# Reordering the head of a fused S5 scan and gated-MLP kernel: load order, held-back weights, tile-wise gate steps

## Chip, cores, metric

The kernel runs on one core of one Trainium2 chip. The metric is device time in microseconds for one execution. TensorE is called PE, VectorE DVE, ScalarE ACT, GpSimd POOL and SyncE SP; SP, ACT and POOL each have a queue on which they issue DMA transfers.

## What is computed

One input `x` of 2048 tokens by 448 channels is normalised; a diagonal complex state-space recurrence (S5) with 448 states runs over the tokens, and a gated MLP with 1792 hidden channels runs beside it. All arrays are bf16.

```python
xn = layernorm(x)                       # over the 448 channels, no scale or shift
# A: S5
dt = exp(log_dt); Lam_bar = exp(dt * Lam)
Bu = xn @ (((Lam_bar - 1) / Lam)[:, None] * B).T
h[t] = Lam_bar * h[t-1] + Bu[t]         # t = 0 .. 2047, complex
s = 2 * real(h @ C.T) + xn * Dskip
# B: gated MLP
g = silu((sigmoid(xn @ w_gate) * (xn @ w_up)) @ w_down)
out = x + s * g
```

## The kernel before

The 2048 tokens are 16 tiles of 128 tokens, in four chunks of 512. For each chunk the kernel does this:

- **Normalise** (`stats`, `chain`, `norm`): batch-norm statistics on DVE (L347, L348), then the reciprocal deviation. For chunk 0 that is a short chain over DVE and ACT (L356 to L359) and a DVE normalisation (L371) with a copy of the first 64 columns behind the last (the seam, L375). For later chunks the deviation is computed on POOL (L362 to L366), the normalisation is on ACT (L378) and the seam copy on POOL (L381).
- **Transpose**: for chunk 0 on PE, seven 128x128 transposes per tile (`pe_transpose`, L400), evacuated by ACT (L402) and DVE (L404) into `xnT`; for later chunks by two DMA transposes per tile on SP's queue (L307).
- **Gate and up steps** (`gu_step`): for each of seven blocks m, 14 matmuls of 64 rows by 512 tokens (L603, L604: both 64-row halves of the array). In chunk 0 all seven gate blocks come first, then the up blocks; a gate block is evacuated by ACT as a tanh (L619) and an up block by DVE (L628), into `hF`. In later chunks gate and up alternate (L622, L632 on ACT, L633 on DVE). Three PSUM slots `gu` go round.
- **Scan** (`b_units`, `ssm_pair`, `ssm_stack`): the input projections (L667) are copied out by ACT (L678), rotated by cosine and sine tables, scanned on DVE (L721, L753) and rotated back. The tables come from `tables`: phases on DVE (L472, L475, L477, L480), sines and cosines on ACT (L484, L486). The phases need `turn`, which `columns` computes from the four parameter vectors: loaded as rows, turned into columns by 16 one-column matmuls (L438), then ACT's exponential (L443) and small POOL steps (L449, L452).
- **Down and output** (`down`, `yout`): the down projection (L782), the output projection (L810), and the store of each tile.

The order of the work is made by a planner (`Plan`). Every piece of work is entered with its engine, a cost, the tiles it reads and those it writes. `solve` works out due times backwards from PE's order and then picks, for each engine, the available piece that is due first; `emit` issues the instructions in the order of planned start. PE's pieces, and the pieces marked `chain` (the loads of each queue), keep the order in which they were entered. So each engine's order is fixed when the kernel is built, and on the chip an engine waits at its next instruction even if a later one could run.

At the start (entered around L322), the loads are: on SP's queue x tiles 0, 1, then 2 and 3 together, two gate-weight blocks, three up-weight blocks, then x tiles 4 to 7 (`load_x(4, 4)`) and the transposed load of B; on ACT's queue two gate blocks and one up block, after a table load; on POOL's queue four vectors, the down weights `wd` and x tiles 8 to 15, each without a condition. The weights of a kind come as four loads: two halves of 64 partitions, each in a block of the first three m (336 KB) and one of the last four (448 KB). PE starts with 12 matmuls on a zero tile (`warm_mm`). Then tile 0 and tile 1 get gate steps of their own for the first three blocks (`g_head`), and tiles 2 and 3 a common one.

Of the kernel before, what the change touches and what calls it, by code (L numbers as in the profile page):

```python
# [18 lines left out]
D = 448  # L19
F = 1792  # L20
# [52 lines left out]
class Plan:  # L73
# [53 lines left out]
    def solve(self, pe_from):  # L127
# [11 lines left out]
        for o in reversed(self.ops):  # L139
            for b, kind in o.suc:  # L140
                x = b.late - self._gap(o, b, kind) - o.cost
                if kind is not None and o.eng != b.eng:
                    x -= 1.5 if o.dma else 0.2
                o.late = min(o.late, x)
# [38 lines left out]
def kernel(  # L183
# [73 lines left out]
    one = sb.tile([1, 1], BF16, name="one")  # L257
    pio2 = sbt("pio2", [1], FP32)
    vrow = hF_raw[0][0:1, 0:2048].rearrange("p (a b) -> p a b", a=4)
# [27 lines left out]
    def load(eng, key, nbytes, o, i, cost=0.45):  # L287
        e = {"SP": Q, "ACT": A, "POOL": G}[eng]
        add(eng, cost, lambda: e.dma_start(out=o, in_=i), w=[key] if not isinstance(key, list) else key,
            dma=nbytes, chain=True)  # L290

    def load_x(t0, n, q="SP"):
        load(q, [("x", t) for t in range(t0, t0 + n)], n * P * D * 2,
             x_all[:, t0:t0 + n, :], x_src[:, t0:t0 + n, :])
# [3 lines left out]
    def load_w(eng, k, half, b):  # L298
# [5 lines left out]
             wsrc[k][:, c0 + m0 * P:c0 + m1 * P].rearrange("(s p) f -> p s f", p=H))  # L304
# [5 lines left out]
    add("POOL", 0.3, lambda: G.memset(warm[:], 0.0), w=["warm"])  # L310
# [3 lines left out]
    add("POOL", 0.1, lambda: G.memset(one[:], 1.0), w=["one"])  # L314
# [6 lines left out]

    add("ACT", 1.3, lambda: A.preload_act_table_set("sqrt_and_others"), w=["sqrttab"], chain=True)  # L322
    load_x(0, 1)
    load_x(1, 1)
    load_x(2, 2)
    load_w("ACT", "g", 1, 0)
    load_w("SP", "g", 0, 0)
    load_w("ACT", "g", 1, 1)
    load_w("SP", "g", 0, 1)
    load_w("ACT", "u", 1, 0)  # L330
    load_w("SP", "u", 0, 0)
    load_w("SP", "u", 1, 1)
    load_w("SP", "u", 0, 1)
    for k, vec in enumerate((A_log_dt, A_Lambda_im, A_Lambda_re, A_Dskip)):
        load("POOL", ("vrow", k), D * 2, vrow[:, k, 0:448], vec.unsqueeze(0), cost=1.0)


    def warm_mm(n):
# [3 lines left out]
        add("PE", 0.35 * n, f, r=["warm"], w=[("gu", 2)])  # L342
# [7 lines left out]
    def chain(t0, n):  # L350
# [4 lines left out]
        if t0 < TPC:  # L355
            add("DVE", 0.09, lambda: V.tensor_single_scalar(out=ve, in_=var, scalar=EPS, op=ALU.add), r=ks("mv"), w=ks("ve"))  # L356
            add("ACT", 0.2, lambda: A.activation(sd, ve, ACT.Sqrt), r=ks("ve") + ["sqrttab"], w=ks("sd"))
            add("DVE", 0.09, lambda: V.tensor_copy(out=meanf[:, t0:t0 + n, :], in_=mean), r=ks("mv"), w=ks("mf"))
# [9 lines left out]
    def norm(t):  # L368
        b = t % NXN
        if t < TPC:  # L370
# [4 lines left out]
            add("DVE", 0.085, lambda: V.tensor_copy(out=xn[b][:, 448:512], in_=xn[b][:, 0:64]),  # L375
# [18 lines left out]
    def pe_transpose(t):  # L394
# [3 lines left out]
        def f():  # L398
            for s in range(7):
                T.transpose(tp[:, s, :], xn[b][:, s * H:s * H + P], ident[:, :])  # L400
        add("PE", 0.43, f, r=[("xn", b), ("xnw", b), "ident"], w=[("acc", a)])
        add("ACT", 0.476, lambda: A.copy(out=xnT[0][:, 0:4, js], in_=tp[:, 0:4, :]),  # L402
            r=[("acc", a)], w=[("xnT", 0, t, "a")])
        add("DVE", 0.27, lambda: V.tensor_copy(out=xnT[0][:, 4:7, js], in_=tp[:, 4:7, :]),  # L404
            r=[("acc", a)], w=[("xnT", 0, t, "b")])
# [23 lines left out]
    def columns():  # L429
        a = next_acc()  # L430
        vps = flat(acc[a][:, 0:16], 4, 4)
        add("POOL", 0.3, lambda: G.tensor_copy(out=vrow[:, :, 448:512], in_=vrow[:, :, 384:448]),
            r=[("vrow", k) for k in range(4)], w=["vroww"])

        def f():
            for k in range(4):
                for i in range(4):
                    T.matmul(vps[:, k, i:i + 1], lhsT=vrow[:, k, i * P:(i + 1) * P], rhs=one[:], start=True, stop=True)  # L438
        add("PE", 1.0, f, r=["vroww", "one"] + [("vrow", k) for k in range(4)], w=[("acc", a)])
        pv = sbt("pv", [4, 4], FP32)  # L440
        add("DVE", 0.1, lambda: V.tensor_copy(out=pv[:], in_=vps[:]), r=[("acc", a)], w=["pv"])
# [7 lines left out]
        tt = lambda o, x, y, op: (lambda: G.tensor_tensor(out=o, in0=x, in1=y, op=op))  # L449
        theta, arg, turn, r_col = C("theta"), C("arg"), C("turn"), C("r")  # L450
        pool(tt(theta[:], dt_b[:], lim, ALU.mult), ["dt", "pv"], ["theta"])
        pool(lambda: G.tensor_single_scalar(out=turn[:], in_=theta[:], scalar=1.0 / TWO_PI, op=ALU.mult),  # L452
# [538 lines left out]
```

## Time and profile before

| | |
|---|---|
| median of 2 runs | 207.5 us (206.95 to 208.05) |
| profiled execution | 206.59 us, its span 204.8 us |
| PE busy | 186.2 us, 91% of the span |
| DVE busy | 160.0 us, 78% |
| ACT busy | 114.6 us, 56% |
| POOL busy | 43.4 us, 21% |
| chain that ended last, by engine | PE 50%, DVE 23%, DMA 13%, ACT 5%, POOL 4% |
| read from HBM, written | 6.66 MB, 1.84 MB |

The profiled execution's time is its span and 1.8 us around it. Busy shares are means over the whole span. Times in views are counted from the start of the span. In the view by stretches a row gives, after the length, the busy time of PE, PE's weight load, DVE, ACT and POOL with instruction counts, then the granted PE clock as a share of full speed, the DMA share and GB/s. In the view by engine a row gives start, duration, engine, line, operation, the tile written and those read, and in brackets the idle time before it with what ended it.

### The profile page before, as it was taken

Reading aid. Unit: us, or ns where it says so; the run is one execution under the profiler, and the core shown is the slowest. Engines: PE = TensorE matmul, PEld = TensorE weight load, DVE = VectorE, ACT = ScalarE, POOL = GpSimd, SP = SyncE. Lnnn points to the kernel's source line nnn. Section 1 sums busy time; section 2 is a strip of 40 time slices with the busy share of each in tenths; the row PEclk is TensorE's granted clock in tenths of the full one; section 3 lists DMA queues with packets and bytes.
Section 4 is the critical chain, followed back from the end, with each engine's and each line's share of the span. In section 5 each row is a group of like instructions: output and inputs, shape, how many; then the busy total and the mean of one; then the engine's idle time right before and its main releaser. Section 6 shows DMA issues by size and latency. Waiting matters only on the chain.

```text
span 204.8 us, 3700 instructions
## 1 busy us (share of the span) xinstructions
PE 186.2 (91%) x1459; PEld 92.5 (45%) x1459; DVE 160.0 (78%) x304; ACT 114.6 (56%) x160; POOL 43.4 (21%) x94
## 2 busy tenths in 40 slices
PE   7267995899799999999699999999999999999992
PEld 2156652434344544444244544444445444455561
DVE  1552539999999999999999999995599799531153
ACT  2114947948999956734935943836537582510330
POOL 8130749677100017007106100000000000000000
PEclk9859999999999999999999999999999999999998
DMA  5999994345400013300311220000000000001002
GB/s 143 235 295 338 223 165 88 74 91 109 89 2 3 0 22 71 78 12 3 73 40 45 48 67 0 3 22 22 0 16 10 0 3 22 22 27 48 0 22 67
DMA packets 26946, 13.32 MB, mean 65 GB/s; under 512 B 19696, under 2 KB 26368, under 8 KB 26928
## 3 DMA queue, kind: packets, MB, share of 16 engines
q1 hardware_dynamic: 24800, 9.41, 21.6%
q0 software_dynamic: 736, 2.53, 3.9%
q10 hardware_dynamic: 1392, 1.15, 2.6%
q8 instruction: 11, 0.18, 0.4%
q14 instruction: 7, 0.06, 0.1%
HBM read 6.66 MB, written 1.84 MB: 41 GB/s over the span
## 4 chain that ended last, share of the span: by engine, by line
PE 50%; DVE 23%; DMA 13%; ACT 5%; POOL 4%; issue 2%; SPq 1%; DVEq 0%; POOLq 0%; ACTq 0%
PE gu L603 18%; DMA x_all<-in_A_x_dram 13%; PE acc L782 10%; PE acc L810 8%; PE gu L782 5%; PE gu L667 4%; DVE wv L721 4%; DVE hF L628 3%; DVE bst L347 2%; ACT sig L622 2%; DVE hF L633 2%; DVE cT L572 2%; POOL rsd L364 1%; PE acc L816 1%; POOL sdb L363 1%
## 5 line engine op out<-in xcount | busy, mean ns | idle before, releaser
L603 PE MATMUL gu<-xnT,wG 64*128 64x512 bf16 (+2 forms) x238 | 47.7, 347 | 5.0 <-DMA wG<-in_B_w_gate_dram 4.1
L603 PE MATMUL gu<-xnT,wU 64*128 64x512 bf16 x196 | 46.5, 376 | 2.4 <-ACT hF L619 2.4
L604 PE MATMUL gu<-xnT,wG 64*128 64x512 bf16 (+2 forms) x238 | 47.7, 347 | 0.0
L604 PE MATMUL gu<-xnT,wU 64*128 64x512 bf16 x196 | 46.5, 376 | 0.0
L782 PE MATMUL acc<-wd,hF 128*128 128x448 bf16 x168 | 33.8, 353 | 0.0
L603 PEld LDWEIGHTS <-wG 64*128 64x128 bf16 x238 | 21.4, 98 | 25.4 <-DMA wG<-in_B_w_gate_dram 4.2
L782 PEld LDWEIGHTS <-hF 128*128 128x128 bf16 x224 | 21.5, 98 | 21.3 <-issue 2.1
L622 ACT ACTIVATE sig<-gu 128x1024 bf16<-128x1024 f32 x21 | 21.5, 1022 | 14.5 <-PE gu L604 12.1
L603 PEld LDWEIGHTS <-wU 64*128 64x128 bf16 x196 | 17.9, 94 | 22.8 <-issue 2.1
L632 ACT CAST ub<-gu 128x1024 bf16<-128x1024 f32 x21 | 21.2, 1009 | 9.2 <-PE gu L604 9.1
L810 PE MATMUL acc<-cT,hT 128*128 128x448 bf16 x105 | 24.3, 353 | 0.0
L721 DVE TENSOR_TENSOR_SCAN wv<-c_r,st,z 128x512 bf16<-128x512 f32 x18 | 23.0, 1280 | 0.2
L604 PEld LDWEIGHTS <-wG 64*128 64x128 bf16 x238 | 21.1, 98 | 1.2 <-issue 1.0
L604 PEld LDWEIGHTS <-wU 64*128 64x128 bf16 x196 | 17.7, 94 | 3.3 <-issue 3.2
L633 DVE TENSOR_TENSOR hF<-sig,ub 128x1024 bf16<-128x1024 bf16 x21 | 14.2, 681 | 5.8 <-ACT ub L632 5.8
L347 DVE BATCH_NORM_STATS2 bst<-x_all 128x6 f32<-128x448 bf16 x16 | 9.4, 616 | 10.0 <-DMA x_all<-in_A_x_dram 10.0
L667 PE MATMUL gu<-xnT,bT 128*128 128x512 bf16 x72 | 16.9, 380 | 0.0
L792 DVE TENSOR_TENSOR g_t<-zb,sigd 128x448 bf16<-128x448 bf16 x16 | 6.1, 386 | 12.8 <-ACT zb L791 12.8
L678 ACT CAST bus<-gu 128x1024 bf16<-128x1024 f32 x12 | 12.1, 1010 | 4.8 <-PE gu L667 4.8
L810 PEld LDWEIGHTS <-hT 128*128 128x128 bf16 x119 | 10.4, 98 | 7.3 <-issue 0.4
L790 ACT ACTIVATE sigd<-acc 128x448 bf16<-128x448 f32 x12 | 6.5, 540 | 12.2 <-PE acc L782 12.2
L378 ACT ACTIVATE xn<-x_all,nmr,rsd 128x448 bf16<-128x448 bf16 x12 | 8.8, 754 | 5.6 <-POOL nmr L366 5.6
(140 smaller groups left out, 278.9 us busy)
## 6 DMA issues: line engine op xcount, KB each, us to landing
out_dram<-o_t SPq DMA_DIRECT2D x15, 112.0 KB, 1.7
wd<-in_B_w_down_dram POOLq DMA_DIRECT2D x1, 1568.0 KB, 13.6
wU<-in_B_w_up_dram SPq DMA_DIRECT2D x2, 448.0 KB, 19.4
x_all<-in_A_x_dram POOLq DMA_DIRECT2D x1, 896.0 KB, 11.4
wG<-in_B_w_gate_dram ACTq DMA_DIRECT2D x1, 448.0 KB, 6.9
wG<-in_B_w_gate_dram SPq DMA_DIRECT2D x1, 448.0 KB, 14.9
x_all<-in_A_x_dram SPq DMA_DIRECT2D x1, 448.0 KB, 19.2
xnT<-xn SPq DMA_TRANSPOSE x24, 2.4
```

Of the source, the lines that this page charges most:

```text
L347: add("DVE", 0.53, lambda: V.bn_stats(out=bst[b][:], in_=x_all[:, t, :]), r=[("x", t)], w=[("bst", b)])
L378: add("ACT", 0.65, lambda: A.activation(xn[b][:, 0:448], x_all[:, t, :], ACT.Identity, bias=nmr[:, t, :], scale=rsd[:, t, :]), r=[("x", t) ...
L603: T.matmul(gu[a][:, 0, ts], lhsT=w_[0:H, s, ms], rhs=x[0:H, s, ts], start=(s == 0), stop=(s == 6))
L604: T.matmul(gu[a][:, 1, ts], lhsT=w_[H:P, (s + 1) % 7, ms], rhs=x[H:P, s, ts], start=(s == 0), stop=(s == 6))
L622: add("ACT", act(1024), lambda: A.activation(sig[b][:], gu[a][:], ACT.Sigmoid), r=[("gu", a), "sinL", "cosL", "sth", "cth"] + [(s, p) for ...
L632: add("ACT", act(1024), lambda: A.copy(out=ub[b][:], in_=gu[a][:]), r=[("gu", a)], w=[("ub", b)])
L633: add("DVE", dve2(1024), lambda: V.tensor_tensor(out=ho, in0=sig[sb_][:], in1=ub[b][:], op=ALU.mult), r=[("sig", sb_), ("ub", b)], w=hk)
L667: T.matmul(gu[a][:, i, :], lhsT=bT[:, kt, i, pt * P:pt * P + P], rhs=x[:, 2 * kt, :], start=False, stop=(kt == 2))
L678: add("ACT", act(1024), lambda u=u, a=a: A.copy(out=bus[u][:], in_=gu[a][:]), r=[("gu", a)], w=[("bus", u)])
L721: dve(1.194, lambda k=k: V.tensor_tensor_scan(out=wv[:, k, :], data0=rb, data1=z[:, k, :], initial=(st[pt][:, k, :] if c else 0.0), op0=AL ...
L782: T.matmul(d, lhsT=hF[c % 2][:, m, h, js], rhs=wd[:, ft, :], start=(ft == 0), stop=(ft == FT - 1))
L810: T.matmul(y, lhsT=hT[c % 2][:, hm, js], rhs=cT[:, cm, c0:c1], start=(i == 0), stop=(i == 6))
```

## The change

The order of the first loads is changed: four single x tiles alternate between SP's and ACT's queue, followed by the four gate-weight loads, alternating too; ACT's table load comes after them. The up weights follow, two loads on SP's queue at once and two on ACT's after the evacuation of transposed tiles 0 and 1. The load of `wd` on POOL's queue is made to wait for the evacuation of up block 1 (`hF` 0, 1) and that of x tiles 8 to 15 for up block 4 (`hF` 0, 4). Gate steps for the first three blocks go tile by tile for all four tiles, and `columns` moves behind them. The statistics of chunks 2 and 3 are entered after chunk 0's gate and up steps.

Smaller edits: work of POOL that another engine waits for gets a due time 1.0 us earlier. The memset of `warm` moves from POOL to DVE, and there are 9 warm-up matmuls instead of 12. For chunk 0 the copy of the mean and the seam copy move from DVE to POOL. The seven transposes of a tile are split into six, which need no seam, and one; tiles 1 to 3 are evacuated by one ACT copy instead of an ACT and a DVE copy. The vectors lie on four partitions instead of one, so that `columns` needs 4 matmuls against the identity instead of 16 against `one`, which goes. The small steps `theta`, `turn` and `arg` move from POOL to DVE.

```diff
@@ Plan.solve
-                    x -= 1.5 if o.dma else 0.2
+                    x -= 1.5 if o.dma else 1.2 if o.eng == "POOL" else 0.2
...
-    one = sb.tile([1, 1], BF16, name="one")
...
-    vrow = hF_raw[0][0:1, 0:2048].rearrange("p (a b) -> p a b", a=4)
+    vrow = hF_raw[0][0:4, 0:512]
...
@@ load, load_x, load_w: a parameter r, what the load waits for
-            dma=nbytes, chain=True)
+            r=r, dma=nbytes, chain=True)
...
-    add("POOL", 0.3, lambda: G.memset(warm[:], 0.0), w=["warm"])
+    add("DVE", 0.2, lambda: V.memset(warm[:], 0.0), w=["warm"])
...
+    for t in range(4):
+        load_x(t, 1, ("SP", "ACT")[t % 2])
+    for b in (0, 1):
+        load_w("SP", "g", 0, b)
+        load_w("ACT", "g", 1, b)
     add("ACT", 1.3, lambda: A.preload_act_table_set("sqrt_and_others"), w=["sqrttab"], chain=True)
-    load_x(0, 1)
-    load_x(1, 1)
-    load_x(2, 2)
-    load_w("ACT", "g", 1, 0)
-    load_w("SP", "g", 0, 0)
-    load_w("ACT", "g", 1, 1)
-    load_w("SP", "g", 0, 1)
-    load_w("ACT", "u", 1, 0)
-    load_w("SP", "u", 0, 0)
-    load_w("SP", "u", 1, 1)
-    load_w("SP", "u", 0, 1)
     for k, vec in enumerate((A_log_dt, A_Lambda_im, A_Lambda_re, A_Dskip)):
-        load("POOL", ("vrow", k), D * 2, vrow[:, k, 0:448], vec.unsqueeze(0), cost=1.0)
+        load("POOL", ("vrow", k), D * 2, vrow[k:k + 1, 0:448], vec.unsqueeze(0), cost=0.8)
+    for b in (0, 1):
+        load_w("SP", "u", 0, b)
...
-        add("PE", 0.35 * n, f, r=["warm"], w=[("gu", 2)])
+        add("PE", 0.43 * n, f, r=["warm"], w=[("gu", 2)])
...
@@ chain, norm (chunk 0)
-            add("DVE", 0.09, lambda: V.tensor_copy(out=meanf[:, t0:t0 + n, :], in_=mean), r=ks("mv"), w=ks("mf"))
+            add("POOL", 0.15, lambda: G.tensor_copy(out=meanf[:, t0:t0 + n, :], in_=mean), r=ks("mv"), w=ks("mf"))
...
-            add("DVE", 0.085, lambda: V.tensor_copy(out=xn[b][:, 448:512], in_=xn[b][:, 0:64]),
+            add("POOL", 0.19, lambda: G.tensor_copy(out=xn[b][:, 448:512], in_=xn[b][:, 0:64]),
...
@@ pe_transpose
-        add("PE", 0.43, f, r=[("xn", b), ("xnw", b), "ident"], w=[("acc", a)])
...
+        add("PE", 0.36, lambda: f(0, 6), r=[("xn", b), "ident"], w=[("acc", a)])
+        add("PE", 0.06, lambda: f(6, 7), r=[("xnw", b), ("xn", b), "ident", ("acc", a)], w=[("acc", a)])
+        if t == 0:
...
+        else:
+            add("ACT", 0.8, lambda: A.copy(out=xnT[0][:, :, js], in_=tp[:, :, :]),
+                r=[("acc", a)], w=[("xnT", 0, t, "a"), ("xnT", 0, t, "b")])
...
@@ columns
-            for k in range(4):
-                for i in range(4):
-                    T.matmul(vps[:, k, i:i + 1], lhsT=vrow[:, k, i * P:(i + 1) * P], rhs=one[:], start=True, stop=True)
+            for i in range(4):
+                T.matmul(vps[:, i, :], lhsT=vrow[:, i * P:(i + 1) * P], rhs=ident[0:4, 0:4], start=True, stop=True)
...
-        tt = lambda o, x, y, op: (lambda: G.tensor_tensor(out=o, in0=x, in1=y, op=op))
+        tt = lambda o, x, y, op: (lambda: V.tensor_tensor(out=o, in0=x, in1=y, op=op))
...
@@ the order of the work
-    warm_mm(12)
+    warm_mm(9)
...
     pe_transpose(0)
+    load_w("ACT", "u", 1, 0, r=[("xnT", 0, 0, "a")])
+    pe_transpose(1)
+    load_w("ACT", "u", 1, 1, r=[("xnT", 0, 1, "a")])
     g_head(0, 1)
-    pe_transpose(1)
+    pe_transpose(2)
     g_head(1, 2)
-    pe_transpose(2)
     pe_transpose(3)
+    g_head(2, 3)
+    for m in range(3):
+        gu_mm(0, "g", m, slots0[m], 3, 4, False)
+        gu_evac(0, "g", m, slots0[m])
     columns()
-    for m in range(3):
-        gu_mm(0, "g", m, slots0[m], 2, 4, m == 0)
-        gu_evac(0, "g", m, slots0[m])
+    gu_step(0, 3)
     tables()
     coeffs()
     load_x(4, 4)
     b_load()
-    load("POOL", "wd", F * D * 2, wd[:], B_w_down.rearrange("(ft p) d -> p ft d", p=P), cost=1.0)
-    load_x(8, 8, "POOL")
-    for t in range(4, 16):
-        stats(t)
...
+    stats_for(1)
+    prepare(1)
+    c_load()
+    for i in range(4, 13):
         gu_step(0, i)
+        if i == 9:
+            load("POOL", "wd", F * D * 2, wd[:], B_w_down.rearrange("(ft p) d -> p ft d", p=P), cost=1.0,
+                 r=[("hF", 0, 1)])
+    load_x(8, 8, "POOL", r=[("hF", 0, 4)])
+    stats_for(2)
+    stats_for(3)
     b_units(0, (0, 1))
```

## The prediction

> **What bounds the kernel now.** I read the page first: slices, then the chain that ended last, then the waits, then the first 30 us in stretches of 5 us and engine by engine. The slices say where to look.
>
> ```profile
> DVE  1552539999999999999999999995599799531153
> PEclk9859999999999999999999999999999999999998
> GB/s 143 235 295 338 223 165 88 74 91 109 89 2 3 0 22 71 78 12 3 73 40 45 48 67 0 3 22 22 0 16 10 0 3 22 22 27 48 0 22 67
> ```
>
> A slice is 5.12 us. DVE is full from slice 7 (about 30 us) on and loose before; the clock is at 0.5 in slice 3; the DMA is busiest in the first five slices. The chain of waits, in order of time, says what DVE waited for.
>
> ```profile
> 9.63 19.17 DMA x_all<-in_A_x_dram
> 28.82 1.15 DVE bst L347 x2
> ...
> 99.30 0.37 PE gu L654
> ```
>
> The load of x tiles 4 to 7, issued at 9.63, lands 19.17 us later and releases DVE's statistics. From there to 99 us nearly every piece is DVE's, then PE's. So the end is set by when DVE's gap-free stream begins, then by PE. The waits show what hung on that load and what held PE earlier.
>
> ```profile
> DVE bst L347 <- DMA x_all<-in_A_x_dram: 10.0, 4, 4.1
> PE gu L603 <- DMA wG<-in_B_w_gate_dram: 4.1, 1, 4.1
> ACT spm L484 <- DVE hT L477: 4.0, 1, 4.0
> PE gu L603 <- ACT hF L619: 2.4, 1, 2.4
> DVE hT L472 <- POOL c_turn L452: 2.2, 1, 2.2
> ```
>
> Columns: us in total, times, longest. Late x delays L347, behind it on DVE L477, behind that ACT's sine (L484), behind that on ACT the last tanh (L619), and behind that PE: one landing stops four engines. Apart from it, the first gate weights hold PE 4.1 us. DVE's own rows give the two places where its stream can move:
>
> ```profile
> 21.71 1.70 DVE L472 TENSOR_SCALAR hT<-wv,c_turn 128x513 f32<-128x513 f32 x4 [2.15 <-POOL c_turn L452]
> 23.33 1.43 DVE L475 TENSOR_SCALAR hT<-hT 128x513 f32<-128x513 f32 x4
> 28.82 1.15 DVE L347 BATCH_NORM_STATS2 bst<-x_all 128x6 f32<-128x448 bf16 x2 [4.07 <-DMA x_all<-in_A_x_dram]
> ```
>
> And the stretches give rates (last column, GB/s) and granted clock (the column before the DMA share):
>
> ```profile
> 0.00:5.00 5.00, 3.69 (x9) 1.34 (x10) 1.02 (x4) 1.49 (x2) 4.38 (x17) 1.00 0.57 141
> 5.00:10.00 5.00, 1.43 (x11) 0.59 (x9) 2.84 (x11) 0.72 (x2) 0.78 (x1) 0.84 1.12 236
> 10.00:15.00 5.00, 3.28 (x49) 2.92 (x50) 3.10 (x15) 0.41 (x2) 1.76 (x3) 0.50 1.08 292
> 15.00:20.00 5.00, 3.34 (x80) 2.96 (x81) 1.15 (x4) 2.19 (x4) 0.20 (x1) 0.98 1.03 333
> ...
> 25.00:30.00 5.00, 5.00 (x49) 2.58 (x46) 1.18 (x3) 3.05 (x4) 2.52 (x6) 1.00 1.40 191
> ```
>
> **Part 1, the order of the loads.** Four x tiles and the first gate blocks are 448 + 672 = 1120 KB, 1.147 MB. The first 5 us moved 0.705 MB and the next went at 236 GB/s, so the bytes are in at 5 + 0.442/0.236 = 6.9 us; the completion of blocks spread over two queues comes after. Bounds for the first gate step: 6.9, and 11.7 as now. I take 8.0, near the lower, because nothing else is queued ahead now. All eight loads (2.064 MB) are in at 10.8. Up weights (1.606 MB) and x tiles 4 to 7 (0.459 MB) follow: at 236 GB/s x 4 to 7 lands at 10.8 + 2.065/0.236 = 19.5 us instead of 28.8; at 191 (the stretch with up weights and x alone) at 21.6, at 292 at 17.9. What makes room is that 1568 KB of down weights and 896 KB of x 8 to 15, now issued at 4.62 and 11.61, go later. SP's two waits for x landings (3.6 us in all) ahead of up loads go too; I price them at nothing, the bytes being the limit. The two up loads on ACT's queue cost it about 0.66 us each (the row of the one there now); ACT is idle 3.25 and 2.10 us ahead of its evacuations then. Without that cover it is 1.3 us. The square-root table load (1.28 us) moves behind four ACT issues (0.7 us each at most): done by about 4.5, so tile 0 is normalised by 5.4, well ahead of the weights.
>
> **Part 2, PE's head.** A gate step for one tile (42 matmuls) took 2.36 us at clock 0.5 (11.68 to 14.04) and 1.45 at full (15.64 to 17.09); seven transposes took 0.93 and, in the pair at full clock, 0.48. The `columns` matmuls, 16 in 0.53 us, become 4: 0.2. From 8.0 at full clock: four gate steps, two transposes, columns = 5.8 + 1.0 + 0.2, so gate step 3 starts at 15.0. At half clock for the first two tiles it is 17.2. The stretches show 0.84, 0.50, 0.98: together 6.8 us at half clock, begun after PE idled. PE is now idle for less (three warm-up matmuls fewer end at about 4.9, transposes fill 5.4 to 7), so I take half of it: 16.4, against 22.03 now, 5.6 us earlier. The Trainium skill, "TensorE: Matmul & The Clock Gate", Part 1, says that one idle window of about 3.4 us halves the clock and one busy window restores it; the trace's 6.8 us are two such windows, and by the rule alone, with no idle window left, the step would start at 15.0, which no run here shows yet.
>
> The seam copies (L375) and mean copies (L358) go from DVE to POOL: 0.18 and 0.14 there, 0.23 to 0.58 for the same seam copy on POOL (L381). The split transposes hide it, six of seven not needing the seam; without that, 0.4 us a tile. The Trainium skill, "GPSIMD Engine Reference", section 3, speaks against the move: it puts POOL at about half DVE's speed for elementwise work; by it alone the four tiles would lose some tenths. The rows agree on the direction, and the head waits for weights meanwhile. One ACT copy per tile instead of ACT then DVE costs nothing: now they run one after the other (0.59 + 0.36), and 896 columns on ACT come to about 1.0.
>
> **Part 3, DVE's stream.** Columns matmuls to L472 now take 18.81 to 21.71 = 2.90. Two POOL steps with their hops (0.57) become two on DVE (0.15 each): 2.6. Columns at 16.2 put L472 at 18.8, 2.9 us earlier. If three tanh (2.84) slip ahead of the exponential on ACT it is 21.6, next to nothing gained. L472 and L475 run 3.04, to 21.8; x 4 to 7 is there by 21.6 in the slower case, so the 4.07 us gap closes. Sum: 2.9 + 4.1 = 7.0 us. PE can follow: it starts 5.6 earlier, and its later waits (2.38, 1.03 and 1.07 in its rows, all on evacuations of this stretch) leave 4.5 more.
>
> **Part 4, what is given back.** Down weights and x 8 to 15 are now issued by POOL behind evacuations of the up steps. The issues took 1.16 and 0.89 us; they now fall into POOL's busy stretch (30 to 49 us), where the tiles' variance chain (L362 to L366) passes through POOL. Behind them wait these chains, then ACT's normalisations, SP's transposes and PE's next chunk. Bounds: 2.05, and 0 (the planner now starts POOL's work 1.0 earlier relative to its due time; it might even gain, since L363 and L364 stand in the chain that ended last); I take 0.5. Two more small DVE steps: 0.3. The rest (warm memset on DVE, `one` gone, vector rows on four partitions) lies in the idle first microseconds. Net 7.0 - 0.8 = 6.2 us. The profiled execution took 206.59 (span 204.8 and 1.8 around it), 0.9 under the median of 207.5, so: **200.4 us**. Own range 197.5 to 203.5 (clock full: -1.4; tanh first: +2.8; POOL chain: -1.5 to +1.5).
>
> **Rivals.** *POOL waits for the evacuation.* In POOL's fixed order the down-weight issue may stand ahead of the variance chain of tiles 6 and 7. That chain would start at 34.29 - 7 = 27.3; the second up evacuation ends at 36.76 - 7 = 29.7, plus 1.16: 3.6 us late. For it: SP's last transpose issue for chunk 1 ends at 46.96 and PE takes them up at 48.45, a margin of 1.5 only. Against: POOL's larger lead. 200.4 + 3.6 = 204.0.
>
> *x 4 to 7 stays late.* The issue of this load alone held SP 8.39 us (9.63 to 18.02), so its queue was full; up weights are still ahead of it. Then only L472 moves: 206.59 - 2.9 + 0.8 = 204.5. Against: one 448 KB load and two x tiles fewer stand on SP ahead of it, and POOL's traffic is gone.
>
> *Slower: x 8 to 15 comes too late.* DVE's statistics of tile 8 stood at 43.17, so 36 after the shift, with the scan work behind them. Down weights issued at 29.7 + 1.2 need 13.6 by their present row (44.5); x, issued by 35.3, needs 11.4 by its row: 46.7, a stall of 10.7 and 211.1 us. It makes the kernel slower from a stall of 7 us (200.4 + 7 is the median). Against: the stretch from 15 to 20 us moved 333 GB/s, by which 2.52 MB take 7.6 us, landing at 38.5: then 2.5 are lost (202.9); and the statistics can be ordered later.
>
> *More than forecast.* Clock full, and POOL's chain (about 4 us in the chain of waits at 92 to 96) shortened by its lead: 200.4 - 1.4 - 2.5 = 196.5.
>
> **How the numbers follow.** Forecast 0.50, POOL wait 0.15, x still late 0.09, x 8 to 15 too late 0.15, more 0.11. About 2% (203.4 and 211.6 here) is what a measurement of this kernel can tell from no change. Faster beyond it: nearly all of the forecast (0.475), the more-case (0.11), a third of the POOL wait (0.05), some of late x (0.02): 0.66. Slower beyond it: the worse half of the late x 8 to 15 (0.09) and a little of the POOL wait: 0.10. Rest 0.24. Range 197.0 to 206.0: it takes in both middle rivals and leaves out about half of the more-case and most of the slower one.
>
> **What would show it.** Right: first gate matmul at 7 to 9 us; L472 at 18 to 20; no DVE wait for x_all over 1 us after 15 us; the L619 wait of PE down from 2.4 to about 1; DVE full from about 19 on. Wrong: DVE or POOL waiting on x_all, wd or L628 between 25 and 45 us; L472 after 21; transposes of chunk 1 ending more than 1 us after PE wants them.

## The result, and the profile after

The changed kernel takes 218.64 us (median of 2 runs, 218.03 to 219.26), against 207.5 before: a ratio of 1.0537 with an interval of 1.0362 to 1.0712. It is slower by 11 us, where 200.4 was forecast and 197.0 to 206.0 given as the range. The profiled span is 216.3 us (204.8 before). Ratios here come from undisturbed runs and medians from all runs of a kernel, so where runs scatter the two need not agree.

In the slices of the page (5.4 us each, counted from 1) DVE is full from slice 13, not from slice 7: it stands still in slices 11 and 12 (54 to 65 us), where the clock has a second dip, and in slice 6 (27 to 32 us), where the DMA too moves nothing at all, as it never did that early before.

```profile
DVE  4514908999009999999999999999689799642144
PEclk9759889998569999999999999999999999999999
GB/s 161 251 192 184 152 0 59 224 136 113 170 110 5 0 0 3 42 85 42 9 79 23 27 75 50 0 3 21 24 0 21 0 3 21 23 24 44 0 23 64
```

The chain that ended last no longer passes through x tiles 4 to 7. It passes through a stop of PE at 21.6 us for which the profile shows no releaser, and then through the issue and the landing of chunk 1's DMA transposes.

```profile
3.18 7.17 DMA hF<-in_A_Dskip_dram
...
21.62 3.13 issue
...
40.75 5.11 SPq L306
45.96 12.62 DMA xnT<-xn
```

The waits say the same. The wait of DVE for x, 10.0 us before, is down to 2.1, all of it for the first tile; in its place PE waits 10.3 us in one piece for chunk 1.

```profile
PE gu L604 <- DMA xnT<-xn: 10.3, 1, 10.3
POOL hF L431 <- DMA hF<-in_A_Dskip_dram: 3.9, 1, 3.9
PE acc L394 <- POOL xn L369: 3.7, 1, 3.7
DVE bst L341 <- DMA x_all<-in_A_x_dram: 2.1, 1, 2.1
```

DVE's rows, engine by engine, show when the gain was lost. The statistics of x 4 to 7 (L341 now) run at 19.46 without a wait, the phases (L473, was L472) start at 22.60 (21.71 before), the first scan (L722) at 46.51 (46.91 before). The third scan, at 55.63 before, comes at 66.32.

```profile
19.46 1.14 DVE L341 BATCH_NORM_STATS2 bst<-x_all 128x6 f32<-128x448 bf16 x2
22.60 1.67 DVE L473 TENSOR_SCALAR hT<-wv,c_turn 128x513 f32<-128x513 f32 x4
46.51 1.23 DVE L722 TENSOR_TENSOR_SCAN wv<-c_r,z 128x512 bf16<-128x512 f32 x1
50.70 1.22 DVE L722 TENSOR_TENSOR_SCAN wv<-c_r,z 128x512 bf16<-128x512 f32 x1
66.32 1.22 DVE L722 TENSOR_TENSOR_SCAN wv<-c_r,z 128x512 bf16<-128x512 f32 x1
```

What the DMA engines did meanwhile stands in the stretches: granted clock, DMA share and GB/s are the last three columns, PE's busy time the first after the length.

```profile
27.00:33.00 6.00, 6.00 (x50) 3.06 (x48) 0.44 (x2) 5.05 (x7) 0.10 (x1) 0.84 0.00 0
33.00:38.00 5.00, 5.00 (x50) 2.63 (x48) 4.70 (x5) 3.67 (x7) 3.61 (x9) 1.00 0.38 68
38.00:44.00 6.00, 5.75 (x40) 2.42 (x36) 6.00 (x12) 2.75 (x6) 3.58 (x9) 1.00 1.03 246
44.00:50.00 6.00, 3.96 (x28) 1.79 (x27) 5.54 (x9) 5.93 (x11) 0.39 (x2) 1.00 1.39 92
50.00:58.00 8.00, 0.00 (x0) 0.00 (x0) 3.67 (x5) 0.95 (x1) 3.84 (x11) 0.68 1.17 129
```

Six microseconds of nothing, and then three kinds of transfer at once: the down weights, issued by POOL at 35.24, x 8 to 15, issued at 40.12, and the eight transposes, which SP issued from 33.38 on for 16.41 us (11.20 before). The engines were busy by the share and moved 92 GB/s, hardly more than the kernel before moved at a share of 0.40 while chunk 1's transposes ran alone:

```profile
36.00:47.00 11.00, 9.97 (x72) 4.62 (x70) 10.87 (x21) 7.68 (x14) 7.90 (x26) 1.00 0.40 85
```

From issue to landing (last column, median us) all three took long; chunk 1's transposes took 2.4 before, the down weights 13.6 and x 11.4.

```profile
wd<-in_B_w_down_dram POOLq DMA_DIRECT2D x1, 1568.0 KB, 12.0
x_all<-in_A_x_dram POOLq DMA_DIRECT2D x1, 896.0 KB, 17.8
xnT<-xn SPq DMA_TRANSPOSE x8, 12.9
```

### The profile page after: what moved, and what is told of

It reads as the page before. It is cut to its first block, busy times and chain, and to the rows that moved or that the text cites. A ratio compares the mean times of both kernels' runs of the same rounds, so it can differ in the third digit from the quotient of the medians.

```text
span 216.3 us, 3751 instructions
## 1 busy us (share of the span) xinstructions
PE 188.6 (87%) x1479; PEld 93.9 (43%) x1486; DVE 159.0 (74%) x298; ACT 115.6 (53%) x160; POOL 42.5 (20%) x96
## 4 chain that ended last, share of the span: by engine, by line
PE 52%; DVE 21%; DMA 9%; POOL 7%; issue 4%; ACT 3%; SPq 3%; POOLq 0%; DVEq 0%; ACTq 0%
PE gu L604 20%; PE acc L783 9%; PE acc L811 7%; DMA xnT<-xn 6%; PE gu L783 5%; PE gu L605 5%; DVE wv L722 4%; DMA hF<-in_A_Dskip_dram 3%; DVE hF L634 3%; SPq L306 3%; PE gu L668 2%; DVE bst L341 2%; POOL sdb L357 2%; ACT ub L633 1%; DVE z L718 1%
## 5 line engine op out<-in xcount | busy, mean ns | idle before, releaser
L604 PE MATMUL gu<-xnT,wG 64*128 64x512 bf16 (+1 forms) x259 | 51.3, 349 | 11.0 <-DMA xnT<-xn 10.3
L605 PE MATMUL gu<-xnT,wG 64*128 64x512 bf16 (+1 forms) x259 | 51.4, 349 | 3.1 <-issue 3.1
L604 PE MATMUL gu<-xnT,wU 64*128 64x512 bf16 x196 | 46.7, 380 | 0.0
L605 PE MATMUL gu<-xnT,wU 64*128 64x512 bf16 x196 | 46.7, 381 | 0.0
L604 PEld LDWEIGHTS <-wG 64*128 64x128 bf16 x259 | 22.7, 102 | 33.6 <-issue 17.8
L604 PEld LDWEIGHTS <-wU 64*128 64x128 bf16 x196 | 18.2, 95 | 19.3 <-issue 3.3
L605 PEld LDWEIGHTS <-wG 64*128 64x128 bf16 x259 | 22.6, 102 | 4.0 <-issue 2.7
L722 DVE TENSOR_TENSOR_SCAN wv<-c_r,st,z 128x512 bf16<-128x512 f32 x18 | 23.0, 1280 | 0.2
L605 PEld LDWEIGHTS <-wU 64*128 64x128 bf16 x196 | 18.1, 95 | 4.5 <-issue 0.2
L668 PE MATMUL gu<-xnT,bT 128*128 128x512 bf16 x65 | 15.3, 379 | 1.1 <-issue 1.1
L679 ACT CAST bus<-gu 128x1024 bf16<-128x1024 f32 x12 | 11.9, 1006 | 2.0 <-PE gu L668 2.0
L629 DVE SCALAR_TENSOR_TENSOR hF<-hF,gu 128x1024 bf16<-128x1024 bf16 x7 | 8.4, 1211 | 4.1 <-PE gu L605 4.1
## 6 DMA issues: line engine op xcount, KB each, us to landing
wU<-in_B_w_up_dram ACTq DMA_DIRECT2D x1, 448.0 KB, 13.6
```

The source lines that it names most:

```text
L604: T.matmul(gu[a][:, 0, ts], lhsT=w_[0:H, s, ms], rhs=x[0:H, s, ts], start=(s == 0), stop=(s == 6))
L605: T.matmul(gu[a][:, 1, ts], lhsT=w_[H:P, (s + 1) % 7, ms], rhs=x[H:P, s, ts], start=(s == 0), stop=(s == 6))
L629: add("DVE", dve1(1024), lambda: V.scalar_tensor_tensor(out=ho, in0=th, scalar=1.0, in1=gu[a][:], op0=ALU.add, op1=ALU.mult), r=[("gu", a) ...
L668: T.matmul(gu[a][:, i, :], lhsT=bT[:, kt, i, pt * P:pt * P + P], rhs=x[:, 2 * kt, :], start=False, stop=(kt == 2))
L679: add("ACT", act(1024), lambda u=u, a=a: A.copy(out=bus[u][:], in_=gu[a][:]), r=[("gu", a)], w=[("bus", u)])
L722: dve(1.194, lambda k=k: V.tensor_tensor_scan(out=wv[:, k, :], data0=rb, data1=z[:, k, :], initial=(st[pt][:, k, :] if c else 0.0), op0=AL ...
```

## Experiments

The kernel before ran beside each group of runs: 206.71, 206.8, 206.53 and 206.43 us. Theory: the held-back loads now run beside chunk 1's transposes, each slows the other, and PE waits. Rivals: the slowdown is in the reordered head; it is PE's stop at 21.6 us; it is POOL's queue, whenever it is used.

For all of these edits: a condition `r` is known to the planner alone. It fixes where a load stands in its engine's order; on the chip the load goes out when the engine reaches it. In the changed kernel POOL issued `wd` at 35.24 while DVE's evacuation of up block 1 ran until 35.69, and x 8 to 15 at 40.12 while that of up block 4 ran until 40.45. So "made to wait" in the change and "behind" in the runs below mean a place in the order, and the issue times are what counts.

**The hold-back alone, in the kernel before (e3).**

```diff
+        if i == 9:
+            load("POOL", "wd", ..., r=[("hF", 0, 1)])
+    load_x(8, 8, "POOL", r=[("hF", 0, 4)])
...
+    stats_for(2)
+    stats_for(3)
```

> The kernel before, with one part of the change alone: down weights wait for up evacuation 1, x 8 to 15 for up evacuation 4, and the statistics of chunks 2 and 3 are entered later. Theory C: the copies now run beside chunk 1's transposes (36 to 48 us); PE waits 5 to 10 us for them and the time is 212 to 218 us, while x 4 to 7 lands several us earlier than 28.8. Theory L: the head is that of before or better, no wait over 2 us, 204 to 208 us.

Measured: 218.57 us, ratio 1.0557 (1.0484 to 1.063): the whole slowdown, with the old head. The first scan comes at 43.70, 3.2 us sooner than before, and then PE waits:

```profile
PE gu L603 <- DMA xnT<-xn: 11.8, 1, 11.8
```

So the new head is not needed for the slowdown: the placing of these loads (with the later statistics that go with it) is enough.

**No hold-back, in the changed kernel (e4):** both loads without a condition.

> The changed kernel, with both POOL loads free of conditions, as before the change: they are issued in the first 12 us. Theory C: PE's wait for chunk 1's tiles is under 2 us; the head is slower than with the hold-back since the copies share the engines with up weights and B's transposes (x 4 to 7 lands after 20 us instead of 17.4); time 204 to 211 us. Theory L: 216 us or more, since the head gets no earlier.

Measured: 210.15 us, ratio 1.0174 (1.0095 to 1.0253). No wait for the transposes, but issued at 5.07 and 11.98 the two loads delay x 4 to 7: its statistics start at 29.13 instead of 19.46, and DVE waits 16.9 us for x in that one piece. Early costs as well, for another reason.

**Both loads planned behind chunk 1's transposes (e1).**

```diff
-                 r=[("hF", 0, 1)])
+                 r=[("xnT", 1, 3, "a"), ("xnT", 1, 3, "b")])
-    load_x(8, 8, "POOL", r=[("hF", 0, 4)])
+    load_x(8, 8, "POOL", r=[("xnT", 1, 3, "a"), ("xnT", 1, 3, "b")])
```

> The changed kernel, with the two POOL loads (down weights and x 8 to 15) conditioned on the last transposes of chunk 1 instead of on up evacuations. Theory C (collision): the two plain copies share the DMA engines with chunk 1's transposes between 35 and 58 us and stretch them; then PE's wait for chunk 1's transposed tiles falls from 10.3 to under 2 us, the last transpose lands within 4 us of its issue, and the time is 207 to 211 us. Theory L (late producers): the transposes are late because ACT's normalisations and PE's head are late; then the wait stays above 7 us and the time is 216 to 219 us.

Measured: 210.61 us (207.11 to 213.54, 10 runs). PE's wait for the transposes falls from 10.3 to 2.3 us (the theory said under 2) and 8 us come back. Not all: issued at 41.6 and 42.8, while SP issued the last of chunk 1's transposes until 43.28, the loads now run beside the transposes of C, which take 8.0 us to land (4.0 before). ACT waits 2.71 us for C, and DVE 2.03 us for ACT's work on it.

```profile
PE gu L604 <- DMA xnT<-xn: 2.3, 1, 2.3
```

**Only x 8 to 15 behind the transposes, and both loads on ACT's queue.**

```diff
# e12
-    load_x(8, 8, "POOL", r=[("hF", 0, 4)])
+    load_x(8, 8, "POOL", r=[("xnT", 1, 3, "a"), ("xnT", 1, 3, "b")])
# e11
-            load("POOL", "wd", ..., r=[("hF", 0, 1)])
+            load("ACT", "wd", ..., r=[("hF", 0, 1)])
-    load_x(8, 8, "POOL", r=[("hF", 0, 4)])
+    load_x(8, 8, "ACT", r=[("hF", 0, 4)])
```

> The changed kernel with x 8 to 15 behind chunk 1's transposes, down weights held back as in the change. It tells which of the two loads collides. Theory C1 (either is enough, the down weights with 1.6 MB more so): PE still waits 4 to 9 us for chunk 1's transposes, 212 to 216 us. Rival C2 (x 8 to 15, issued last, is the one that runs beside the transposes): the wait is under 2 us and the time about 210, as with both behind the transposes.

> The changed kernel (218.64 us) with the two held-back loads issued on ACT's queue instead of POOL's, under the same conditions. Theory C (any plain copy on a second queue beside SP's transposes slows both): PE waits 5 to 12 us for chunk 1's transposes as in the changed kernel, 214 to 220 us. Rival P (it is POOL's queue, or POOL's own work behind the issue, that does it): the wait is under 2 us and the time 206 to 211.

Measured: 207.1 us (201.94 to 209.86, 10 runs) and 207.42 (205.61 to 211.14, 12 runs). In the first, with the down weights at 34.34 beside the transposes and x at 42.24, PE still waits 4.5 us for them, as C1 said, but the time misses C1's 212 to 216 and the runs scatter by 8 us. That x makes up the rest of the 10.3 is likely, not shown. The second gave the numbers of the rival, not those of the theory: PE does not wait for chunk 1. But it is no clean test. ACT stood before the second load until 46.0 (the bracket names what came last before its next instruction), so x went out only when most of chunk 1's transposes had been issued; and PE then waited 3.07 us for the copies of ACT (L679) that stood behind that load.

```profile
46.02 0.41 ACTq L288 DMA_DIRECT2D x_all<-in_A_x_dram  x1
46.47 1.33 ACT L487 ACTIVATE cosT<-hT,pio 128x512 bf16<-128x512 f32 x2 [5.70 <-DMA xnT<-xn]
```

After these, two readings stood: the time at which the loads run, or POOL's queue. The down weights alone leave room for the second: they went out beside the same transposes in both runs, landed after 7.4 us on ACT's queue and after 11.1 on POOL's, and only on POOL's did PE wait (though there x too ran beside the last of them).

**The same queue, released earlier (e13).** Both loads stay on POOL's queue, but are planned behind the tanh of gate block 3, so that POOL issues them at 26.34 and 27.55, ahead of and in the six empty microseconds.

```diff
+    def held():
+        G.dma_start(out=wd[:], ...)
+        G.dma_start(out=x_all[:, 8:16, :], ...)
+    add("POOL", 2.0, held, w=["wd"] + [("x", t) for t in range(8, 16)], r=[("hF", 1, 3)], ...)
...
-            load("POOL", "wd", ..., r=[("hF", 0, 1)])
-    load_x(8, 8, "POOL", r=[("hF", 0, 4)])
```

> The changed kernel (218.64 us) with both held-back loads still on POOL's queue, but released by the tanh of gate block 3 instead of by up blocks 1 and 4: POOL issues them one behind the other right behind the variance chain of tiles 6 and 7, at about 27 us, when the DMA engines stand idle, and before chunk 1's transposes (33 us). Theory C (what costs is that these loads run beside the transposes): PE's wait for chunk 1's transposes goes from 10.3 us to under 2, the loads land within 8 to 10 us of their issue, time 205 to 209. Rival P (POOL's queue or its issue is what costs, whenever it comes): wait over 4 us, time 212 or more.

Measured: **201.92 us** (200.76 to 206.58, 4 runs), ratio 0.9716 (0.9632 to 0.9799). 16.7 us less than the change as made, by a release 9 and 13 us earlier, and below the 205 to 209 that the theory gave. The issues and the stretches of this run:

```profile
wd<-in_B_w_down_dram POOLq DMA_DIRECT2D x1, 1568.0 KB, 7.9
x_all<-in_A_x_dram POOLq DMA_DIRECT2D x1, 896.0 KB, 10.3
xnT<-xn SPq DMA_TRANSPOSE x8, 6.8
```

```profile
27.00:33.00 6.00, 6.00 (x58) 3.21 (x56) 5.12 (x6) 4.32 (x8) 3.25 (x9) 1.00 0.78 254
33.00:38.00 5.00, 4.10 (x30) 1.87 (x27) 5.00 (x8) 1.90 (x5) 3.34 (x9) 1.00 1.15 264
38.00:44.00 6.00, 5.30 (x36) 2.30 (x35) 5.54 (x12) 5.95 (x9) 0.38 (x1) 1.00 1.10 106
44.00:50.00 6.00, 5.67 (x48) 2.88 (x49) 5.93 (x9) 4.84 (x7) 4.86 (x12) 1.00 0.79 153
```

The loads go at 254 and 264 GB/s and are in by 37.9; PE's wait for chunk 1 is down to 0.7 us. SP issues chunk 1's transposes from 28.79 on, so part of them still runs beside x: they take 6.8 us to land instead of 2.4, but are wanted later than that. So on one queue the time of release alone takes the slowdown away: POOL's queue is not dear whenever it is used. Whether another queue would be cheaper at the bad time is a question that this run does not touch. The median is the lowest of all the kernels here, though 0.27 us ahead of e16 below is less than the runs scatter.

**The loads on SP's queue, behind B's transposes,** in the changed kernel (e5) and in the one before (e8): issued at 26.8 and 27.5, ahead of chunk 1's transposes in one queue.

```diff
     b_load()
+    load("SP", "wd", 16, wd[:], ...)
+    load("SP", [("x", t) for t in range(8, 16)], 16, x_all[:, 8:16, :], ...)
```

> The changed kernel, with down weights and x 8 to 15 issued on SP's queue between B's transposes and chunk 1's, with no condition: one queue, so no plain copy runs beside a transpose of another queue, and the DMA's empty stretch of the changed kernel (27 to 33 us) takes them. Theory C: both loads land by 37 us, chunk 1's transposes land within 4 us of their issue, PE's wait for them is under 2 us, and C's transposes are not stretched either; 204 to 208 us, less than the run with the copies moved behind chunk 1's transposes. Rival (any late copy of this size costs the same, whatever runs beside it): chunk 1's transposes queue behind 2.5 MB and PE waits over 5 us again, 212 us or more.

> The kernel before, with only down weights and x 8 to 15 moved from POOL's queue to SP's, behind B's transposes. Theory C: x 4 to 7 lands at 20 to 23 instead of 28.8 us, as with the hold-back, but no copy runs beside chunk 1's transposes; DVE's scans start about 3 us earlier and the time is 202 to 205 us. Rival (x 4 to 7 is not what binds): 206 to 208 us.

Measured: 205.32 us, ratio 0.9888 (0.9805 to 0.9971), and 204.84, ratio 0.9892 (0.982 to 0.9965). The same release time on another queue again removes PE's wait. That the two agree says that the rest of the change brought nothing yet, which sends the search to its head.

**The seam copies of chunk 0 back on DVE,** in the changed kernel (e2) and in e5 (e16).

```diff
-            add("POOL", 0.19, lambda: G.tensor_copy(out=xn[b][:, 448:512], in_=xn[b][:, 0:64]),
+            add("DVE", 0.085, lambda: V.tensor_copy(out=xn[b][:, 448:512], in_=xn[b][:, 0:64]),
```

> The changed kernel, with the four seam copies of chunk 0 back on DVE. Both theories: the first gate matmul moves from 11.2 us to 8 or 9, because the seam copy no longer stands on POOL behind the copy that waits for the vector loads (10.4 us). Theory C: the gain ends at PE's wait for chunk 1's tiles, so the time stays within 2 us of 218.6. Theory L: an earlier head is an earlier end, 214 to 216 us.

> The run with both loads on SP's queue (205.32 us) with the seam copies of chunk 0 on DVE again, and nothing else. Theory S (the seam on POOL delays tile 0's last transpose by 3 us behind the vector rows and is not hidden): first gate matmul at 8 to 9.5 us instead of about 11, time 202.5 to 204.5. Rival (the head has slack there): within 0.5 us of 205.3.

Measured: 212.67 us (206.36 to 213.63, 4 runs, too scattered for a ratio) and 202.19, ratio 0.9753 (0.9675 to 0.983). The first lies below what both theories gave for it: with the loads at 35.01 and 39.74, nearly as in the changed kernel, PE waits 6.9 us for chunk 1 and not 10.3, so the price of the overlap is not one number. The second is 3.1 us under e5, though the two intervals overlap. With the seam on POOL PE's last transpose of tile 1 waited 4.14 us for it (e5); now the first gate matmul, at 11.2 us in the changed kernel, stands at 8.05 and waits for the weights:

```profile
8.05 0.28 PE L604 MATMUL gu<-xnT,wG 64*128 64x128 bf16 x1 [0.31 <-DMA wG<-in_B_w_gate_dram]
```

In the changed kernel the same place reads as below. POOL runs in order, and ahead of its seam copy (L369) stood a copy that waits for the vector rows (L431, 3.9 us in the list of waits).

```profile
10.96 0.29 PE L394 MATMUL acc<-ident,xn 128*128 128x128 bf16 x1 [3.70 <-POOL xn L369]
```

**B's transposes planned behind the up weights** (e6 in the changed kernel, e7 together with e16's edits).

```diff
-            tload([("bT", i)], bT[:, 0:3, i, :], m[:, 0:384], D * 768)
+            tload([("bT", i)], bT[:, 0:3, i, :], m[:, 0:384], D * 768, r=[("w", "u", h, m_) ...])
```

> The changed kernel, with B's transposes made to wait for the up weights, so that they don't run beside the up loads of ACT's queue; the hold-back and the seam copies stay as changed. Theory F (instruction fetch): PE's 3.1 us stall at 21.6 us, inside an accumulation group, is PE waiting for its instructions, whose fetch is slow beside transposes and copies; then the stall falls under 1 us and the half clock from 25.7 us is gone. Rival: the stall is something else on PE and stays at 2.5 to 3.5 us. In both cases the collision with chunk 1's transposes remains, so the time is 214 to 219 us.

> The changed kernel with three mends at once: copies on SP's queue between B's and chunk 1's transposes, seam copies on DVE, B's transposes after the up weights. If the three losses named by the traces are the whole difference between forecast and result (PE's wait 10.3, seam 3.7, PE's stall 3.1 and half a clock window 1.7, partly hiding each other), the head is 4 to 6 us ahead of the kernel before and the time is 200 to 204 us. If something else binds (DVE's stream or ACT's order in the head), it is 205 us or more.

Measured: 210.88 us (203.66 to 214.21, no ratio), and 203.11, ratio 0.9809 (0.9756 to 0.9861). SP's issue of B's transposes began at 5.64 all the same, ahead of ACT's two up loads: on SP's queue nothing stands between, and the condition alone holds nothing on the chip.

```profile
5.64 11.21 SPq L306 DMA_TRANSPOSE bT<-in_A_B_re_dram  x2
12.17 1.32 ACTq L288 DMA_DIRECT2D wU<-in_B_w_up_dram  x2
```

So e6 did not separate what it was to separate (PE's stop was 2.10 us, between its theory and its rival), it can only have moved other pieces in the plan, and e7 is no faster than e16, which lacks the edit. PE's wait for chunk 1 in e6 is 8.4 us, again not 10.3.

**The columns earlier,** ahead of the third tile's gate steps, so that ACT's exponential stands ahead of the three tanh (e9: e7 with this; e10: without the condition on B; e14: e9 with the planner told the size of the two loads, which moves the later statistics behind the first scans).

```diff
     pe_transpose(3)
+    columns()
     g_head(2, 3)
...
-    columns()
     gu_step(0, 3)
```

> The changed kernel with down weights and x 8 to 15 on SP's queue behind B's transposes, the seam copy of chunk 0 on DVE, B's transposes made to wait for the up weights, and now the columns entered after the transposes of tile 3 and before the gate steps of tile 2, so that ACT's exponential stands ahead of the three tanh. The same without the last edit took 203.11 us, with the phases' first step on DVE behind tanh and statistics. Theory T (the prediction's step for the phases was lost to the tanh standing ahead of the exponential, and DVE's stream sets the end): the first phase step starts 2 to 3.5 us earlier, at about 19, before the statistics of tiles 4 to 7, the scans start 1 to 3 us earlier and the time is 200.5 to 202. Rival U (the order on ACT is not what sets the scans; projections of chunk 0 or the statistics come last there): the phase step moves, the scans stay at 41.5 within 0.5, time 202.6 to 203.6. Rival V (tanh behind the exponential delays PE's third gate step and its up steps): 204 or more.

> As the run with the columns ahead of the third gate steps, but B's transposes are issued without a wait for the up weights, as in the changed kernel. Theory C (DMA transposes beside plain copies on another queue slow both; so ACT's two up loads suffer beside B's transposes): 0.3 to 1.5 us slower than the run with the wait, with a stall of PE in the up steps or a later x 4 to 7. Rival (the up weights have slack, and the wait does nothing): within 0.3 us of it.

> As the run with the columns ahead of the third gate steps (206.27 us), but the planner is told the size of the two loads on SP's queue, so that it puts the statistics of tiles 8 and later behind the first scans instead of among the up steps. Theory W (the 6 us by which the phases came sooner were lost to DVE's wait for x tile 8 and to the statistics put ahead of the scans): first scan at 38 to 40.5 us instead of 44.6, time 199 to 202.5. Rival (the scans wait for something else, such as the projections' evacuation on ACT or the tables): first scan stays after 42 and the time is 203 or more.

Measured: 206.27 us, ratio 0.9962 (0.9922 to 1.0001); 208.25, 1.0055 (1.0018 to 1.0092); 205.65, 0.9924 (0.988 to 0.9967). All miss what the theory wanted, and all are slower than e7 at 203.11; e9 has the time that rival V gave (204 or more). In e10 B's transposes start at 5.61, in e9 at 5.85, so the 2 us between these two come from other shifts in the plan and say nothing of B. The phases come 6 us earlier, and in e9 DVE uses it to wait for x tile 8, which the planner had put before the scans:

```profile
16.45 1.77 DVE L473 TENSOR_SCALAR hT<-wv,c_turn 128x513 f32<-128x513 f32 x4
35.91 0.63 DVE L341 BATCH_NORM_STATS2 bst<-x_all 128x6 f32<-128x448 bf16 x1 [3.28 <-DMA x_all<-in_A_x_dram]
44.61 1.22 DVE L722 TENSOR_TENSOR_SCAN wv<-c_r,z 128x512 bf16<-128x512 f32 x1
```

With those statistics behind the scans (e14) the first scan stands at 41.45, which is where e7 has it (41.46) with phases five microseconds later. What sets it there is PE: its gate step after the tile-wise ones waits for the tanh, now behind the exponential and two table loads, and then runs at half clock (0.50 at 20 to 22 us); DVE in turn waits 1.65 us for the first projection's copy. Why e14 ends 2.5 us behind e7 from the same first scan was not followed up.

```profile
19.62 0.58 PE L604 MATMUL gu<-xnT,wG 64*128 64x512 bf16 x1 [3.04 <-ACT hF L620]
```

**Six warm-up matmuls in PE's gap** ahead of the first gate weights (added to e7).

```diff
             f(6, 7)
+            for _ in range(6 if t == 1 else 0):
+                T.matmul(gu[2][:, 0, :], lhsT=warm[:, 0:P], rhs=warm[:], start=True, stop=True)
```

> As the run with the loads on SP's queue, the seam on DVE and B's transposes behind the up weights (203.11 us), with six more warm-up matmuls behind the transposes of tile 1, where PE waits 1.68 us for the first gate weights. Theory H (PE's gap there brings the half clock of 6.83 us): no half clock between 9 and 16 us, third gate step for tile 3 done about 3 us sooner, but the next gate step then waits for the tanh; time 200.5 to 203. If the clock is halved all the same, the gap is not its cause and the time stays within 0.5 us of 203.1.

Measured: 203.69 us, ratio 0.9795 (0.9713 to 0.9876): nothing gained on e7. The half clock is shorter (3.41 us instead of 6.83) and comes later, but is not gone. After six matmuls PE reaches its next gap (2.15 us, waiting for tile 2's normalisation) and the clock is halved from 12.66 to 16.07 us:

```profile
8.00:10.00 2.00, 2.00 (x46) 1.27 (x43) 0.35 (x3) 0.32 (x1) 0.00 (x0) 1.00 1.13 233
10.00:12.00 2.00, 0.02 (x2) 0.00 (x0) 0.28 (x1) 0.00 (x0) 0.48 (x3) 1.00 1.12 201
12.00:14.00 2.00, 1.83 (x33) 1.73 (x35) 1.10 (x6) 0.53 (x2) 0.00 (x0) 0.66 1.13 195
14.00:16.00 2.00, 2.00 (x33) 1.61 (x29) 0.00 (x0) 0.59 (x2) 0.00 (x0) 0.50 1.13 200
```

## Why the prediction was wrong, and where it was right

**The step that failed is Part 4, what is given back.** It priced the held-back loads by POOL's issue alone: between 0 and 2.05 us, 0.5 taken. What the place of these loads cost is read from pairs of kernels whose edits differ in it (e3 and e8 also in where the later statistics are entered): 16.7 us (changed kernel, 218.64, less e13, 201.92), 13.3 (less e5), 10.5 (e2 less e16) and, in the old head, 13.7 (e3 less e8). The prediction had the rows for it, 13.6 and 11.4 us to land, and used them for one reader only, DVE's statistics of tile 8. It did not lay them beside the other traffic of 35 to 58 us, SP's transposes of chunk 1, though it had PE's margin there as 1.5 us. An estimate from the rows of the changed kernel adds up to the 17.3 us by which its span is longer than that of e13: 10.3 of waiting, 2.2 for the half clock behind it (58.71 to 63.04), 3.1 for PE's stop at 21.6 and 1.7 for the half clock behind that (25.49 to 28.90). The first two, 12.5 us, are put down to the overlap; the stop is taken up under "Open". Put in order of release, the same two loads gave:

| issued at (us) | queue | beside what | time (us) |
|---|---|---|---|
| 5.1, 12.0 | POOL | up weights, x 4 to 7, B's transposes | 210.15 |
| 26.3, 27.6 | POOL | an idle stretch | 201.92 |
| 35.2, 40.1 | POOL | chunk 1's transposes | 218.64 |
| 41.6, 42.8 | POOL | C's transposes | 210.61 |

The Trainium skill, "DMA: Bandwidth & Descriptors", section "Rules for kernel authors", says that a transpose next to ordinary DMAs needs nothing. The sentence stands in a row on corrupted data and is no statement on time, where this case shows a price: 12.9 us to land instead of 2.4.

**The slower rival had the length of the stop nearly right, by luck, and the place wrong.** It put the landing of x 8 to 15 at 46.7 and a stop of 10.7 us on DVE. The load landed at 57.9, later still; but DVE's statistics had been ordered behind the scans, and PE stopped first, for 10.3 us and for another cause. The rival of a POOL that waits for the evacuation could not come true as told: POOL does not wait for it, it issues the load when its turn comes.

**The forecast of the rest was near, in part by luck.** With the loads released in the idle stretch the profiled execution takes 200.76 us, the median 201.92, against 200.4. But the terms of the sum did not all come:

- *The 4.1 us of x 4 to 7*: the landing right. It lands 12.0 us after its issue at 5.37, so at 17.4 where 19.5 was said (17.9 to 21.6 by the bounds), and the gap is gone. What that is worth in time is smaller: in the old head (e8), where the gap goes too and little else changes, the first scan comes 3.1 us sooner and the time falls by 2.0 us. The gain of e13, 206.43 less 201.92 = 4.5 us, is near 4.1, but it is not shown to be this term.
- *The phases, 2.9 us*: wrong twice. The bound "three tanh slip ahead" (21.6) is what happened: 22.60, and 22.09 in e13, later than the 21.71 before. And where the phases did come early (16.45 in e9 and 17.21 in e14), no time was gained; in e14 PE's steps come last before the first scan, so the term is not on the path there.
- *First gate matmul at 8.0*: the loads were priced about right (8.05 in e9 and e16, 8.5 to 9.2 in e14, e2, e10 and e7), the seam copies wrong. "The split transposes hide it" looked at what PE does and not at what POOL has ahead of the copy; the price given for the cover gone, 0.4 us a tile, became a wait of 3.70 us and 3.1 us of the time. The copy itself takes 0.24 us on POOL and 0.18 on DVE, so POOL's speed was the small part.
- *Half of the 6.8 us at half clock*: in the changed kernel it was the whole, 8.43 to 15.26. With gaps of 0.57 and 0.31 us ahead of the first gate weights (e9, e16) the gate steps of the four tiles run at full clock; with 1.68 (e7) it is halved from 8.91 to 15.74, again 6.83 us. But the length of the gap alone does not decide it (see the last section). Gate step 3 started at 19.96 (16.4 forecast), 18.04 in e16; in both rows it is the tanh that releases it, after 0.70 us.

Two of the three signs named as "wrong" came true: the phases after 21, and chunk 1's transposes more than 1 us late. DVE and POOL did not wait for x, `wd` or the evacuations, as the first sign had it. Of the signs named as "right", two came: no wait of DVE for x after 15 us, and PE's wait for the tanh down to 0.70 us.

**Open.** PE's stop of 3.13 us at 21.6 inside a group of matmuls, with no semaphore behind it, shows in some kernels and not in others (2.72 in e1, 3.82 in e2, 2.10 in e6, 4.20 in e11, 2.39 in e12, 2.17 in e16; none in e3, e5 and e13). A 16 KB packet on an instruction queue (q8) comes in near it (1.3 us long at 22.0 in the changed kernel, 2.0 us long at 18.6 in e16), but kernels without the stop have one too (1.2 us long at 18.1 in e13), and none was moved on purpose: that the fetch of instructions is the cause is only argued. By the estimate above the stop and its half clock are at most 4.8 of the 17.3 us. It is neither needed for the slowdown nor enough for it: e3 has none and takes 218.57 us, e16 has one and takes 202.19. And whether the same overlap on ACT's queue would be as dear was not settled by e11.

## What to carry to other kernels

A load that is held back is not free because its reader has time: write down what else the DMA engines do in the stretch that it moves into, transposes above all, and who waits for that. Look for a stretch in which the DMA moves nothing, and release the load there; here one lay eight microseconds ahead of the point that was chosen. A gain on an engine counts only after asking which wait comes last once it is there: the phases came six microseconds sooner and the scans did not. And a condition that only the planner knows is an order, not a wait: read from the trace when the load really goes out.

## What the runs showed of the hardware

- Plain loads on POOL's queue beside DMA transposes on SP's: from 44 to 50 us of the changed kernel the two together moved 92 GB/s at a share of 1.39, some 38 of it the transposes (0.23 MB) and 52 the loads (0.31 MB). The transposes alone moved 85 GB/s at 0.40 in the kernel before, and in e13 the plain loads with few transposes beside them went at 254 to 264. Both are slower together than each alone. But the overlap is not the only thing that makes a row like this: in e13 from 38 to 40 us, when both plain loads had landed, the transposes left over moved 66 GB/s at a share of 1.53. The Trainium skill, "DMA: Bandwidth & Descriptors", section "Queues, rings and completion order", says that each DMA engine takes turns between queues packet by packet. That fits a transpose standing behind large packets; by itself it does not give the low total, which no run here explains.

```profile
38.00:40.00 2.00, 1.80 (x11) 0.61 (x10) 1.65 (x7) 2.00 (x3) 0.38 (x1) 1.00 1.53 66
```

- The granted clock falls for 3.41 us (e15, 12.66 to 16.07), for twice that (e7 and e13, 6.83) or three times (the changed kernel, 52.80 to 63.04). Within one run the changes lie multiples of 3.41 us apart (the changed kernel: 8.43, 15.26, 25.49, 28.90, 52.80, 63.04). The length of PE's gap does not foretell a fall: in the 3.41 us ahead of the fall in e15 PE still ran for 1.26 (first row below), while in e12 it stood for 4.39 us (second row) and the clock stayed at 1.00, before and after. The Trainium skill, "TensorE: Matmul & The Clock Gate", Part 1, speaks of an idle window of about 3.4 us; the lengths agree, but in e15 a window idle for two thirds was enough. What decides was not tested.

```profile
9.25:12.66 3.41, 1.26 (x35) 0.98 (x29) 0.64 (x3) 0.21 (x1) 0.48 (x3) 1.00 1.13 208
7.70:12.10 4.40, 0.01 (x2) 0.01 (x1) 0.97 (x5) 0.00 (x0) 0.47 (x3) 1.00 1.12 216
```
